# New transpose forms for the q, k, tail and output layouts of a fused attention and channel-mix kernel, with refitted scheduler constants

## Chip, cores and metric

One core of a Trainium2 chip. The metric is the device time of one execution in microseconds (us); medians over the runs of one call. All runs quoted are of the fast state, but for one slow run in f3's median; spans and granted clocks are those of the one core.

## The reference, cut to what matters

```python
# q, k, v: (8 batches, 8 heads, 576 rows, 64), float32
scores = scale * q @ k.T + alibi_bias                  # per batch and head
mask   = (rel >= 0) & (rel < 128)                      # sliding window of 128
attn   = softmax(where(mask, scores, -1e9)) @ v
x      = attn.transpose(0, 2, 1, 3).reshape(8, 576, 512)
# channel mix: x shifted by one row and mixed, then
xk, xr = mu_k * x + (1 - mu_k) * x_prev, mu_r * x + (1 - mu_r) * x_prev
out    = sigmoid(xr @ w_r) * (relu(xk @ w_k) ** 2 @ w_v)
```

## The kernel before

It works on head pairs: 4 groups g in each of 8 batches b. For each pair q and k must be turned so that the head dimension lies on the partitions; scores, exponential (ScalarE), mask (VectorE) and the product with v follow; the attention output must be turned again for the channel mix. A turn is done by TensorE (a transpose is a matmul with the identity, followed by a copy from PSUM) or by the DMA crossbar (a "flip").

The kernel does not list its instructions in their order. It makes a graph of operations, each with a modelled duration, priority, buffers and engines, and a greedy list scheduler orders every engine from these models while the program is built. The built program then holds each engine's instructions in that order.

```python
# the scheduler, cut: an engine that is free takes the first candidate whose buffers are free
if e == "PE":
    cand.sort(key=lambda n: self.pe_key(n, rows))
...
for n in cand:
    if self.take(n):
        break
...
# fitted constants of the schedule
XB = range(5, B)          # q and k of these batches by crossbar
XO = range(6, B)          # attention output of these by crossbar
WIDE = (1,)               # q and k of these by 64x64 quarter transposes
QM, OM = 0, 1             # q, k: full transposes; output: half-height ones
XD, WAIT, XRL = 6, 2.0, 3.0
A = {PE: 14.25, ACT: 4.00, DVE: 4.50, VIR: 0}     # lead of attention over channel mix

# PSUM: two double banks for scores ("duo"), four single ones for all else ("uno")
duo = [pst.tile([128, 2, 512], FP32, name=f"duo{i}") for i in range(2)]
uno = [pst.tile([128, 512], FP32, name=f"uno{i}") for i in range(4)]

# scores of one head pair: two halves, each takes one double bank and is freed by one exponential
s = op(PE, ..., need + [x[5] for x in todo], free)
x = op(ACT, act_t(2 * w), [s], ..., nc.scalar.activation(out=ah(), in_=two(hp)..., func=AF.Exp), (), [hp])

# q and k, full transposes: 8 of 128x128, one single bank, one copy of 1024 columns
def qk_full(b, g, prio):
    hp, hq = Hold(PT), Hold("qk")
    ...
    y = op(ACT, act_t(1024), [t], prio + (3,), lambda e: copy_any(e, qk_buf[hq.idx]..., one(hp)...), (), [hp])

# q and k, quarter transposes: 2 * nr * 4 of 64x64, two single banks, two copies
def qk_quad(b, g, nr, buf, deps, prio, c0, hq, take, free):
    hp = [Hold("p1"), Hold("p1")]
    ...
    ys = [op(QK0 if b == 0 else ACT, {...}, [t], prio + (3,), ..., (), [hp[r]]) for r in range(2)]

# output, half-height transposes: 10 for a head pair, two single banks, two copies (320 + 256)
def out_some(b, g, hx, deps, prio, ht): ...
```

The softmax here doesn't subtract the row's maximum and nothing guards it: scores larger than these inputs give would overflow.

Of the kernel before, what the change touches and what calls it, by code (L numbers as in the profile page):

```python
# [179 lines left out]
def kernel(  # L180
# [12 lines left out]
    nc = tc.nc  # L193

    B, H, S, D = q.shape
    DM = H * D
    DF = moe_w_k.shape[1]
    G = H // 2
    NF = S // 128
# [7 lines left out]
    SM = 128 * NF  # L207
    RELU_SCALE = 0.5 ** 0.5

    PE, ACT, DVE, POOL, SPE, FAB, VIR = "PE", "ACT", "DVE", "POOL", "SP", "FAB", "VIR"  # L210
    NQ, NA, NX, NV, NC = 4, 4, 3, 2, 2
    XB = range(5, B)
    XO = range(6, B)
    X0 = 16
    NWARM = 90
    LOADS = 'v23KtVkabcRWw'
    XD = 6
    OTL = 1.5
    FIN = 384
    RATE = 284.0  # L220
    WIDE = (1,)
    PART_WIDE = True
    QUAD = 0.0565
    RUN = {2: 64 * 284 / 329.0, NF: 128 * 284 / 357.0}
    FLIP = 1.25
    NO = 5
    WAIT = 2.0
    QM = 0
    OM = 1

    def XU(b, g):
        return (DVE,)
# [1 line left out]
    def SQ(order):  # L234
        return (DVE,)

    XT0 = (ACT,)
    QK0 = (ACT, DVE)
    CAST = (DVE,)
    FT = (2, 3)  # L240
    KQ = ACT
    VCUT = True
    XTT = range(6, B)
    MMASK = False
    VDEP = 1
    TCOST = 1.5
# [14 lines left out]
    ts_buf = many(2, [128, H, D], BF16, "ts")  # L261
    tt_buf = many(2, [128, G, 3, 64], BF16, "tt")
# [23 lines left out]
    ident = cst.tile([128, 128], BF16, name="ident")  # L286
# [16 lines left out]
    def one(h):  # L303
        return uno[h.idx if h.cls == "p1" else N1 + h.idx]

    def two(h):
        return duo[h.idx]

    plan = Plan(dict(qx=2, xb=2, p2=2, p1=N1, pt=4 - N1, qk=NQ, at=NA, xu=NX, vs=NV, cb=NC, ts=2, tt=2, xt=2, dl=2, dl0=4,
                     xk=2, rl=3, kk=3, rs=4, ot=NO),  # L310
                {}, WAIT)
# [8 lines left out]
    def dve_t(n, fast=1):  # L320
        return (n / fast + 66) / 960.0

    AHEAD = 30.0
    A = {PE: 14.25, ACT: 4.00, DVE: 4.50, VIR: 0}
    NBIAS = 4
    XRL = 3.0
    MODE = 0
    EARLY = 0.0
    SLOPE = 4.5
# [12 lines left out]
    def op(e, dur, deps, prio, emit, need=(), free=()):  # L342
        prio = rank(prio)
        return plan.add(e, dur, LAT.get(e, 0.2) if isinstance(e, str) else LAT[e[0]] if len(e) == 1 else 0.22,
                        deps, prio, emit, need, free)

    last = {}

    def virtual(key, holds):
        n = plan.add(VIR, 0.0001, 0.0001, [last.get(key)], (0,), None, holds)  # L350
        last[key] = n
        return n
# [11 lines left out]
    def dma(queue, kb, issue, emit, deps=(), need=(), free=(), lat=(1.0, 0.9)):  # L364
        n = plan.add(queue, issue, 0.0, list(deps) + [last.get(queue)],
                     (len(plan.nodes),), emit, need)
        last[queue] = n
        return fab(queue, kb / RATE, n, lat, free)
# [38 lines left out]
    n_ident = dve_op(0.11, emit_ident, [n_iota], (0, -1))  # L407
# [21 lines left out]
    def issue_t(nd):  # L429
        return 0.53 + 0.00034 * nd  # L430
# [16 lines left out]
    def tail_load(b):  # L447
        h = Hold("ts")
        g = virtual("ts", [h])
        ns = []  # L450
        for i in range(2):
            src = (q, k)[i][b, :, SM:S].rearrange("h p d -> p h d")
            ns.append(dma(POOL, 128 * TCOST, issue_t(512), lambda e, i=i, src=src: nc.gpsimd.dma_start(
                out=ts_buf[h.idx][64 * i:64 * i + 64], in_=src), [g]))
        return h, ns
# [66 lines left out]
    th, tl, n_w, src1 = {}, {}, {}, {}  # L522
# [31 lines left out]
    cw, ch, cl, xbh, xbl, tth, ttl, ttg = {}, {}, {}, {}, {}, {}, {}, {}  # L554
# [42 lines left out]
    for (c0, n) in DSEG:  # L597
        n_copy[c0] = dve_op(dve_t(n, 4), lambda e, c0=c0, n=n: nc.vector.tensor_copy(
            out=dist[:, c0:c0 + n], in_=dist[:, 0:n]), [n_dist], (0, 1))
    n_sid = [dve_op(0.1, lambda e, h=h: nc.vector.tensor_scalar(  # L600
        out=sid[:, h], in0=ident, scalar1=-(2.0 ** (-(h + 1))) / scale, scalar2=None,
# [6 lines left out]
    def emit_mu(e):  # L608
# [5 lines left out]
        out=mu_sb.rearrange("p i o -> p (i o)"), in_=one(h_mu)[:, 0:2 * NPO]), (), [h_mu])  # L614
# [12 lines left out]
    def copy_any(e, out, in_):  # L627
        (nc.scalar.copy if e == ACT else nc.vector.tensor_copy)(out=out, in_=in_)  # L628
# [213 lines left out]
            res.append(fab(SPE, 1.0 * rows / 128, n, (1.0, 0.9), [hx]))  # L842
        return res

    def tails(b, prio):
        htt = Hold("tt")
        hs = th[b]
        if b in XTT:
            plan.follow(last["tt"], ttg[b])
            last["tt"] = ttg[b]  # L850
            return tth[b], ttl[b]
        hp = Hold("p1")

        def emit(e):
            for g in range(G):
                nc.tensor.transpose(  # L856
                    one(hp).bitcast(BF16)[:, 128 * g:128 * g + 128],
                    ts_buf[hs.idx][:, 2 * g:2 * g + 2].rearrange("p h d -> p (h d)"), ident)

        def emit_c(e):  # L860
            copy_any(e, tt_buf[htt.idx][:, :, 0:2].rearrange("p g t c -> p g (t c)"),
                     one(hp).bitcast(BF16)[:, 0:128 * G].rearrange("p (g w) -> p g w", g=G))

        t = op(PE, 0.0565 * G, list(tl[b]) + [n_ident], prio + (0,), emit, [hp], [hs])
        g = virtual("tt", [htt])
        c = [op(DVE, dve_t(512), [t, g], prio + (0,), emit_c, (), [hp])]
        return htt, c


# [152 lines left out]
    for part in range(2):  # L1022
        if part == 1:
            htt, n_tt = tails(0, (0, 0, 1, 0))
        for g in range(G):
            prio = (0, 0, part, g)
# [12 lines left out]
            hp = Hold("p1") if part == 0 else None  # L1039
# [29 lines left out]
            for j, (pieces, m0) in enumerate(PART[part]):  # L1069
# [8 lines left out]
            r, hx = attend(0, g, t0, t1, ha, es + vl[0][0:2] + (vl[0][2:] + blank if part else []),  # L1078
                           prio)
# [171 lines left out]
```

## Time and profile before

| | before |
|---|---|
| median of the given runs | 234.99 us (234.88 to 235.05) |
| profile span | 233.1 us |
| TensorE busy | 225.8 us (97%) |
| VectorE, ScalarE busy | 189.8, 160.8 us |
| granted clock | 1.00 |

Matmuls overlap in the pipeline (one of 512 columns is recorded as 380 ns long, and the next starts 216 ns after it), so busy time is not a sum of costs. Throughout I use one account instead. The **priced work** is the sum, over all TensorE groups in their built order, of start-to-start times that the trace shows when nothing waits (216 ns for 512 columns, 109 for 256, 56 for 128, 0.28 us for 32 quarter transposes, 0.16 for ten half ones, 0.25 for a group of the new tail form, 93 ns for each change of array form). The **gaps** are the rest from TensorE's first start to its last, with the last matmul's own price: waits of any kind, and slow matmuls. For the kernel before: 228.8 us = 218.9 priced + 9.95 of gaps.

### The profile page before, as it was taken

What the parts mean: (1) busy time and instruction counts of PE and PEld (TensorE: products, weight loads), DVE (VectorE), ACT (ScalarE), POOL (GpSimd) and SP (SyncE); (2) the same over time, 40 slices, a digit from 0 to 9 for tenths busy, and PEclk for the clock granted to TensorE, in tenths of its full rate; (3) what the DMA queues carried; (4) which work ended last, traced back from release to release, by engine and by line L of the source; (5) the groups of instructions that cost most, each with busy time, mean ns of one, the idle gap of its engine ahead of it and who ended that gap; (6) DMA issues with size and microseconds to landing.
All of it is one profiled execution on the core that took longest, in us unless ns stands there. A gap on an engine that the chain in (4) does not pass through costs nothing.

```text
span 233.1 us, 6268 instructions
## 1 busy us (share of the span) xinstructions
PE 225.8 (97%) x2487; PEld 135.7 (58%) x2487; DVE 189.8 (81%) x427; ACT 160.8 (69%) x292; POOL 97.7 (42%) x124
## 2 busy tenths in 40 slices
PE   7899989999999999999999999999999999999994
PEld 6576765556566765555555755455655844455462
DVE  7587988987797989989989979985769996974242
ACT  3669999759999986984984975947584726326251
POOL 8966773898883893069508935200000000000000
PEclk9999999999999999999999999999999999999999
DMA  7999999999999999989999999993232124121122
GB/s 168 178 167 196 161 162 185 153 199 201 155 154 173 109 138 207 106 106 169 201 188 100 172 181 211 155 146 106 69 89 93 45 48 146 46 90 48 65 70 90
DMA packets 131100, 31.73 MB, mean 136 GB/s; under 512 B 120056, under 2 KB 127232, under 8 KB 131072
## 3 DMA queue, kind: packets, MB, share of 16 engines
q0 software_dynamic: 102736, 16.26, 102.7%
q1 hardware_dynamic: 26592, 14.50, 26.9%
q10 hardware_dynamic: 1744, 0.59, 1.0%
q8 instruction: 19, 0.31, 0.5%
q14 instruction: 9, 0.07, 0.1%
HBM read 33.56 MB, written 9.44 MB: 184 GB/s over the span
## 4 chain that ended last, share of the span: by engine, by line
PE 84%; ACT 5%; DMA 3%; POOL 3%; issue 2%; DVE 1%; DVEq 0%; POOLq 0%; ACTq 0%
PE uno L941 27%; PE uno L907 26%; PE uno L925 14%; PE duo L716 6%; PE duo L658 5%; DMA ts<-in_k_dram 3%; PE uno L771 2%; PE uno L1154 2%; ACT at L672 2%; POOL qx L434 1%; ACT mask L1088 1%; ACT qk L628 1%; PE uno L856 1%; POOL vs L438 1%; ACT rl L914 1%
## 5 line engine op out<-in xcount | busy, mean ns | idle before, releaser
L941 PE MATMUL uno<-wv_sb,kk 128*128 128x512 bf16 (+2 forms) x296 | 71.8, 374 | 0.0
L907 PE MATMUL uno<-xk,wk_sb 128*128 128x256 bf16 (+2 forms) x416 | 69.5, 314 | 0.7 <-ACT rl L914 0.4
L672 ACT ACTIVATE at<-duo 128x1024 bf16<-128x1024 f32 (+2 forms) x68 | 65.7, 1002 | 5.4 <-PE duo L658 5.4
L914 ACT ACTIVATE rl<-uno 128x256 bf16<-128x256 f32 (+2 forms) x104 | 47.3, 492 | 20.3 <-PE uno L907 19.0
L907 PEld LDWEIGHTS <-wk_sb 128*128 128x128 bf16 x416 | 38.7, 98 | 22.1 <-issue 0.9
L685 DVE TENSOR_TENSOR at<-at,mask 128x1024 bf16<-128x1024 bf16 x56 | 37.7, 680 | 8.2 <-ACT at L672 7.8
L438 POOL DMA_DIRECT2D vs<-in_v_dram x32 | 28.4, 895 | 33.9 <-PE duo L716 30.3
L941 PEld LDWEIGHTS <-kk 128*128 128x128 bf16 x296 | 26.4, 98 | 26.2
L880 DVE TENSOR_TENSOR kk<-rl 128x256 bf16<-128x256 bf16 (+2 forms) x104 | 32.8, 334 | 9.0 <-ACT rl L914 7.8
L932 ACT ACTIVATE rs<-uno 128x512 bf16<-128x512 f32 x36 | 22.1, 614 | 26.1 <-PE uno L925 23.1
L925 PE MATMUL uno<-wr_sb,xr 128*128 128x512 bf16 x144 | 37.0, 379 | 0.5 <-ACT rl L914 0.5
L946 DVE SCALAR_TENSOR_TENSOR ot<-rs,uno 128x512 f32<-128x512 bf16 (+2 forms) x37 | 24.6, 668 | 12.1 <-PE uno L941 9.7
L716 PEld LDWEIGHTS <-at 128*128 128x128 bf16 x576 | 21.8, 98 | 6.0 <-issue 0.9
L821 DVE SCALAR_TENSOR_TENSOR xk<-dl,mu_sb,xt 128x576 bf16<-128x576 bf16 (+1 forms) x32 | 24.8, 780 | 0.4
L821 DVE SCALAR_TENSOR_TENSOR xr<-dl,mu_sb,xt 128x576 bf16<-128x576 bf16 (+1 forms) x32 | 24.4, 769 | 0.0
L463 POOL DMA_DIRECT2D cb<-in_k_dram x24 | 21.3, 901 | 7.1 <-DMA wv_sb<-in_moe_w_v_dram 3.3
L628 ACT COPY xt<-uno 128x256 bf16<-128x256 bf16 (+1 forms) x48 | 17.1, 405 | 9.0 <-PE uno L771 8.8
L925 PEld LDWEIGHTS <-xr 128*128 128x128 bf16 x144 | 13.5, 98 | 14.6 <-issue 0.7
L463 POOL DMA_DIRECT2D cb<-in_q_dram x24 | 21.2, 915 | 1.4 <-DMA vs<-in_v_dram 1.2
L628 ACT COPY qk<-uno 128x1024 bf16<-128x1024 bf16 (+2 forms) x26 | 18.8, 777 | 2.4 <-PE uno L1049 0.8
L716 PE MATMUL duo<-vs,at 128*128 128x65 bf16 x448 | 19.1, 193 | 0.0
L814 DVE TENSOR_TENSOR dl<-xt 128x576 bf16<-128x576 bf16 (+1 forms) x32 | 13.7, 434 | 4.2 <-ACT xt L628 4.2
(78 smaller groups left out, 206.8 us busy)
## 6 DMA issues: line engine op xcount, KB each, us to landing
out_dram<-ot SPq DMA_DIRECT2D x30, 256.0 KB, 5.2
vs<-in_v_dram POOLq DMA_DIRECT2D x32, 128.0 KB, 6.6
cb<-in_q_dram POOLq DMA_DIRECT2D x24, 128.0 KB, 7.0
cb<-in_k_dram POOLq DMA_DIRECT2D x24, 128.0 KB, 6.8
out_dram<-ot SPq DMA_DIRECT2D x10, 128.0 KB, 1.8
wk_sb<-in_moe_w_k_dram POOLq DMA_DIRECT2D x2, 512.0 KB, 8.8
wv_sb<-in_moe_w_v_dram POOLq DMA_DIRECT2D x2, 512.0 KB, 10.8
qx<-in_k_dram ACTq DMA_DIRECT2D x4, 128.0 KB, 4.5
```

The source lines that it names most:

```text
L438: return dma(POOL, 256, issue_t(1024), lambda e: nc.gpsimd.dma_start(out=vs_buf[h.idx][:, j, :, 0:D], in_=v[b, :, 128 * j:128 * j + 128].r ...
L463: return [dma(POOL, 256, issue_t(1024), lambda e, r=r: nc.gpsimd.dma_start(out=cb_buf[h.idx][:, i, r], in_=src[:, :, r]), [g]) for r in ra ...
L628: (nc.scalar.copy if e == ACT else nc.vector.tensor_copy)(out=out, in_=in_)
L672: lambda e, ah=ah, w=w, hp=hp: nc.scalar.activation(out=ah(), in_=two(hp)[:, :, 0:w], func=AF.Exp, scale=float(scale)), (), [hp])
L685: nc.vector.tensor_tensor(out=a, in0=a, in1=m, op=ALU.mult)
L716: nc.tensor.matmul(a[:, hl, t - t0], lhsT=at[:, lo:lo + 128], rhs=vs[:, u, 2 * g + hl, :] if u < NF else tvb[:, 2 * g + hl], start=(u == u ...
L821: lambda e: nc.vector.scalar_tensor_tensor(out=buf[hk.idx][:, g, e0 + c0:e0 + c1], in0=dls(), scalar=mu[:, g:g + 1], in1=xc(1), op0=ALU.mu ...
L880: nc.vector.tensor_tensor(out=out, in0=in_, in1=in_, op=ALU.mult)
L907: nc.tensor.matmul(one(hp)[:, 0:n], lhsT=wk_sb[:, po, 128 * fo:128 * fo + 128], rhs=xk_buf[hx.idx][:, po, c0:c1], start=(po == 0), stop=(p ...
L914: a = op(ACT, act_t(n), [s], pr, lambda e, hp=hp, hr=hr: nc.scalar.activation(out=rl_buf[hr.idx][:, 0:n], in_=one(hp)[:, 0:n], func=AF.Rel ...
L925: nc.tensor.matmul(one(hp), lhsT=xr_buf[hx.idx][:, po, 128 * c:128 * c + 128], rhs=wr_sb[:, po], start=(po == 0), stop=(po == NPO - 1))
L941: nc.tensor.matmul(one(hv)[:, a:b], lhsT=kk_buf[hk.idx][:, fo, o:o + 128], rhs=wv_sb[:, fo, a:b], start=(fo == 0), stop=(fo == NFO - 1))
```

## The change

The intent: cheaper q and k loads (512-byte instead of 128-byte pieces) and quarter transposes for batches 1 to 4; full instead of half transposes for the output of these batches; the output of batch 5 moved from TensorE to the crossbar; tails of batches 0 and 1 loaded head-major and turned by 16 matmuls; and refitted constants for the scheduler. The diff, cut:

```diff
-    XO = range(6, B)
+    XO = range(5, B)
-    XD = 6
+    XD = 4
-    WIDE = (1,)
+    WIDE = (1, 2, 3, 4)
+    TW = (0, 1)
-    QUAD = 0.0565
-    RUN = {2: 64 * 284 / 329.0, NF: 128 * 284 / 357.0}
+    QUAD = 0.040
+    RUN = {2: 64 * 284 / 345.0, NF: 128 * 284 / 390.0}
-    WAIT = 2.0
-    QM = 0
-    OM = 1
+    WAIT = 1.0
+    QM = 1
+    OM = 0
-    XT0 = (ACT,)
+    XT0 = (ACT, DVE)
-    XTT = range(6, B)
+    XTT = range(5, B)
-    A = {PE: 14.25, ACT: 4.00, DVE: 4.50, VIR: 0}
+    A = {PE: 10.75, ACT: 10.00, DVE: 3.00, VIR: 0}
-    XRL = 3.0
+    XRL = 4.0
# tail_load: batches in TW are loaded as "h (c r) d -> h c (r d)", r=4
# tails(), for batches in TW:
+            for n in range(8):
+                for hl in range(2):
+                    nc.tensor.matmul(
+                        one(hp)[64 * hl:64 * hl + 64, 64 * n:64 * n + 64],
+                        lhsT=ts_buf[hs.idx][:, n],
+                        rhs=ident.rearrange("p (g t c) -> p t g c", g=G, t=2)[:, hl],
+                        start=True, stop=True)
# ... and two VectorE copies of 256 in place of one of 512 (cut)
```

More of the change, by code (lines that the diff above doesn't have):

```diff
@@ L450, in tail_load @@
         ns = []
+        if b in TW:
+            for i in range(2):
+                ns.append(dma(POOL, 104, issue_t(128), lambda e, i=i: nc.gpsimd.dma_start(
+                    out=ts_buf[h.idx].rearrange("p h d -> p (h d)")[:, 256 * i:256 * i + 256],
+                    in_=(q, k)[i][b, :, SM:S].rearrange("h (c r) d -> h c (r d)", r=4)), [g]))
+            return h, ns
         for i in range(2):
@@ L843, in out_flip, with tails_full @@
         return res
-    def tails(b, prio):
-        htt = Hold("tt")
-        hs = th[b]
-        if b in XTT:
-            plan.follow(last["tt"], ttg[b])
-            last["tt"] = ttg[b]
-            return tth[b], ttl[b]
+    def tails_full(b, prio, htt, hs):
         hp = Hold("p1")
@@ L866, in tails, with emit @@
         c = [op(DVE, dve_t(512), [t, g], prio + (0,), emit_c, (), [hp])]
+        return htt, c
+    def tails(b, prio):
+        htt = Hold("tt")
+        hs = th[b]
+        if b in XTT:
+            plan.follow(last["tt"], ttg[b])
+            last["tt"] = ttg[b]
+            return tth[b], ttl[b]
+        if b not in TW:
+            return tails_full(b, prio, htt, hs)
+        hp = Hold("p1")
+        def emit(e):
+            for n in range(8):
[5 more added lines that the diff above has]
+                        start=True, stop=True)
+        t = op(PE, 0.03 * 16, list(tl[b]) + [n_ident], prio + (0,), emit, [hp], [hs])
+        g = virtual("tt", [htt])
+        c = [op(DVE, dve_t(256), [t, g], prio + (0,), lambda e, i=i: copy_any(
+            e, tt_buf[htt.idx][:, :, i].rearrange("p g (c r) -> p g c r", r=4),
+            one(hp)[:, 256 * i:256 * i + 256].rearrange("p (r g c) -> p g c r", r=4, g=G)),
+                (), [hp]) for i in range(2)]
         return htt, c
```

## The prediction

> **What bounds the kernel now.** I read the page first: busy time by engine, then the windows table, then the groups by form on PE and ACT, the chain that ended last, and the PE timeline.
>
> ```profile
> PE 225.8 (97%) x2487; PEld 135.7 (58%) x2487; DVE 189.8 (81%) x427; ACT 160.8 (69%) x292; POOL 97.7 (42%) x124
> ```
>
> PE is busy for 225.8 of 233.1 us, and the granted clock is 1.00 in every window. The chain that ended last is 84% PE. So the time is the sum of what PE issues, plus its gaps. The windows say where gaps can be (PE, PEld, DVE, ACT, POOL busy, then clock, DMA share, GB/s):
>
> ```profile
> 0.00:20.00 20.00, 18.03 (x264) 12.42 (x264) 14.98 (x64) 12.14 (x23) 15.87 (x27) 1.00 1.52 174
> 20.00:40.00 20.00, 18.18 (x363) 13.88 (x358) 16.75 (x46) 19.19 (x45) 12.45 (x15) 1.00 1.79 174
> 60.00:80.00 20.00, 20.00 (x272) 13.48 (x271) 17.50 (x39) 18.66 (x34) 14.40 (x18) 1.00 2.05 148
> ```
>
> From 40 us on PE is full; before that it lacks about 4 us, and in 20 to 40 us ACT is at 19.19 of 20. The first 25 us also hold 90 filler matmuls. Busy time of pipelined matmuls overlaps, so I cost everything by start-to-start times, which the timeline shows:
>
> ```profile
> 32.35 0.45 PE L1002 MATMUL uno<-ident,cb 64*64 64x64 bf16 x32
> 32.73 1.05 PE L907 MATMUL uno<-xk,wk_sb 128*128 128x256 bf16 x8
> ...
> 38.89 0.32 PE L771 MATMUL uno<-ident,xu 64*128 64x64 bf16 x10
> 39.14 1.04 PE L925 MATMUL uno<-wr_sb,xr 128*128 128x512 bf16 x4
> ...
> 40.97 0.32 PE L771 MATMUL uno<-ident,xu 64*128 64x64 bf16 x10
> 41.13 0.55 PE L658 MATMUL duo<-qk 64*128 64x256 bf16 x8
> ```
>
> Ten half-height output transposes (one head pair) cost 0.16 us when another 64-row form follows (40.97 to 41.13), and 0.25 when a 128-row form follows (38.89 to 39.14): a change of array form costs 0.09 us. Thirty-two quarter transposes, what batch 1 already uses for q and k, take 0.38 with such a change at the end, so 0.29 without.
>
> ```profile
> 66.15 0.61 PE L1154 MATMUL uno<-ident,cb 128*128 128x128 bf16 x8
> 66.60 0.39 PE L856 MATMUL uno<-ident,ts 128*128 128x128 bf16 x4
> 66.82 1.06 PE L1154 MATMUL uno<-ident,cb 128*128 128x128 bf16 x16
> ```
>
> Eight full transposes take 0.45 us, four take 0.22: 56 ns each.
>
> **What the Trainium skill says.** (1) "TensorEngine Tiling (Array Packing)", Key Properties: changing the tiling mode drains TensorE. The trace agrees and gives the size: over all 106 changes of form in the kernel before, the interval exceeds the steady one by a median of 90 to 96 ns by kind of change. (2) "TensorE: Matmul & The Clock Gate", Wait — 56ns, not 53.3ns: a warm matmul costs N / 2.4 GHz plus about 2.5 ns. The trace agrees: median start-to-start is 216 ns at 512 columns, 109 at 256, 56 at 128. (3) Same page, Part 3: matmuls in different tiles of the array overlap, with starts about 4 ns apart. The trace agrees: in a quarter-transpose group three starts follow at 3 to 4 ns, then one at 22. (4) "DMA: Bandwidth & Descriptors", Specifications: at least 512 B is wanted for line rate. The trace's packet records agree in direction: 128 B packets of the software queue took a mean of 35.3 ns, 512 B ones 60.7, so four small ones cost 141 for the bytes of one.
>
> **The change, part by part.** Group counts are from the order of instructions in the two built kernels.
>
> q and k of batches 2 to 4: 12 groups (3 batches, 4 head pairs) of 8 full transposes become 32 quarter ones. 12 x (0.29 - 0.45) = -1.9 us of PE.
>
> Output of batches 1 to 4: 16 groups of ten half transposes become five full ones: 16 x (5 x 0.056 - 0.16) = 16 x 0.12 = +1.9 us.
>
> Output of batch 5: its 4 groups leave PE for the crossbar: -4 x 0.16 = -0.6 us. Its tail transposes leave too: -0.2 us.
>
> Tails of batches 0 and 1: four full transposes (0.22) become 16 matmuls of 64 columns with two column tiles. No row of the trace has this form; if pairs overlap as in (3), 8 pairs at 31 ns (the half transposes' pitch) are 0.25, so +0.05 us in all; if they don't, 16 at 29 ns, +0.5.
>
> Changes of form: 106 before, 110 after: +4 x 0.093 = +0.4 us. The half transposes often sat next to scores in the 64-row form, and the full ones do not; the quarter ones need a form of their own.
>
> Sum on PE: -1.9 + 1.9 - 0.6 - 0.2 + 0.05 + 0.4 = about -0.4 us. Summing every group of both orders with the same prices, unrounded, gives 218.9 and 218.4 us, so -0.5. **The TensorE part is nearly a wash.** The kernel before issued over 228.6 us, so it holds about 9.7 us of gaps over this sum; some 7.5 of these fall before 40 us, including 1.3 of slow first fillers.
>
> ACT, from its groups by form:
>
> ```profile
> L628 ACT COPY qk<-uno 128x1024 bf16<-128x1024 bf16 x12 | 11.9, 1042 | 0.7 <-PE uno L1154 0.7
> L628 ACT COPY xt<-uno 128x320 bf16<-128x320 bf16 x24 | 10.1, 428 | 8.8 <-PE uno L771 8.8
> L628 ACT COPY xt<-uno 128x256 bf16<-128x256 bf16 x24 | 9.1, 382 | 0.3 <-DVE qk L628 0.2
> L628 ACT COPY qk<-uno 128x512 bf16<-128x512 bf16 x10 | 5.7, 619 | 0.8 <-PE uno L1049 0.8
> ```
>
> q and k: 12 x (2 x 0.619 - 1.042) = +2.4 us. Output of batches 1 to 4: 0.428 + 0.382 = 0.81 becomes one copy of 576; by the slope between 512 and 1024 columns I estimate 0.67, so 16 x -0.14 = -2.2. Batch 5: -4 x 0.81 = -3.2. Batch 0: the order shows five of its eight output copies moved to VectorE and one 256-column q/k copy back: -2.0 + 0.4. Sum -4.6 us. Most is beside PE's work and worth nothing. Only the 1.6 us of batch 0 lie in the first 30 us, where ACT is what PE waits for; I count a third to a half, 0.5 to 0.8 us. VectorE gets about 2 us more there, at 15 to 17 of 20 busy: enough room, but less than before.
>
> DMA: a batch of q and k is 8192 packets of 128 B before, 2048 of 512 B after: 8192 x 35.3 / 16 = 18.1 against 7.8 us of engine time. As the DMA share is near 2 when full, wall time is half: 5 us less for each of three batches. This is the largest number here, and I give it nothing: after 40 us PE's list of waits names no DMA. It buys headroom only. The tails of batches 0 and 1 go from 1024 to 256 packets, 2.26 to 0.97 us by the same sum, 0.65 in wall time each. The first is on the chain that ended last:
>
> ```profile
> 8.60 8.04 DMA ts<-in_k_dram
> 18.08 1.30 ACT at L672 x2
> ```
>
> Landing at 16.6 it gates the scores of batch 0's second part. I count half of 0.65, since two VectorE copies follow in place of one and nine fillers now stand just behind in PE's order.
>
> Total: 234.99 - 0.5 (PE) - 0.65 (ACT early) - 0.3 (tails) = 233.5. The priorities and rates of the scheduler were refitted as well, presumably to shorten early gaps, so I shade to **233.3 us**.
>
> **Rivals.** (a) The crossbar becomes a wait. The before kernel flips outputs of batches 6 and 7 when q/k flips are over; now batch 5's five flips (about 1.25 us each on the issuing queue) stand before most of batch 7's q/k flips in an in-order queue, while loads still run. If a flip waits for the last output of batch 5, batch 7's scores come late and PE, in fixed order, stops for 1 to 4 us: 234.5 to 237. For it: the queue order. Against it: these flips land in 2.4 us, and the loads finish some 15 us of DMA time earlier, so the flips start earlier. (b) The freed DMA time does matter, because earlier q and k let attention run ahead and fill the gaps of 20 to 40 us: at most some 3 us of gaps there vanish, 230.5 to 231.5. Against: ACT at 96% limits that window, not loads. (c) Two half-size copies in place of one, with two PSUM banks per quarter-transpose group, make PE wait for a bank: say 12 groups by 0.1 to 0.2, 235 to 236. Batch 1 ran so and did show stalls of 0.4 and 0.5 us behind its groups, but in the ACT-bound window.
>
> **Range and chances.** The counted PE sum is firm to about 0.5 us; the early gaps can give up to 2 us more than I count, and (a) or (c) can cost 2. So 231.5 to 235.3. Faster by 2% needs 230.3, more than half of all gaps gone: 0.04. Slower by 2% needs 4.7 us of new stalls: 0.03. Within 2%: 0.93.
>
> **What would show it right or wrong.** Right: groups of 32 quarter transposes at about 0.29 us apart from the form change, five full ones at 0.28, PE busy about 0.5 us less, the DMA share well below 2 from 40 to 120 us, ACT under 158 us, no wait of PE on DMA after 40 us. The gain, if any, should lie before 40 us: the same point of the channel mix reached about 1 us earlier, and the stretch from there to the end shorter by under 1 us. Wrong: PE waits on crossbar flips, or 20 us windows after 60 with PE under 19.8; tail matmuls at over 0.5 us a group; a gain over 3 us, which would mean that loads had held the early part.

## The result, and the profile after

| | before | changed |
|---|---|---|
| median | 235.02 us (234.88 to 235.27, 4 runs) | 235.99 us (235.78 to 236.21, 4 runs) |
| ratio to before | | 1.0040, 95% interval 1.0023 to 1.0058 |
| profile span | 233.1 | 234.4 |
| priced TensorE work | 218.9 | 218.4 |
| gaps | 9.95 | 11.8 |
| ScalarE, VectorE busy | 160.8, 189.8 | 157.6, 190.6 |

A ratio here is the mean time of one kernel's fast runs over the mean of the other's of the same rounds, so not quite the ratio of the medians. The changed kernel is 0.4% slower: within 2%, as predicted, but on the other side of zero and outside the range (231.5 to 235.3).

First the page's busy line, then the windows (columns as in the prediction: PE, PEld, DVE, ACT, POOL busy, clock, DMA share, GB/s), both of the changed kernel:

```profile
PE 223.9 (96%) x2645; PEld 137.2 (59%) x2675; DVE 190.6 (81%) x432; ACT 157.6 (67%) x276; POOL 85.4 (36%) x112
```

```profile
0.00:20.00 20.00, 18.02 (x273) 13.24 (x273) 15.07 (x66) 10.76 (x20) 15.92 (x27) 1.00 1.47 174
20.00:40.00 20.00, 17.72 (x360) 12.79 (x356) 16.94 (x49) 17.95 (x40) 11.32 (x15) 1.00 1.67 180
40.00:60.00 20.00, 19.27 (x362) 12.87 (x365) 19.40 (x38) 17.61 (x30) 12.91 (x17) 1.00 1.82 195
60.00:80.00 20.00, 18.87 (x341) 11.93 (x343) 17.95 (x37) 18.38 (x32) 10.65 (x14) 1.00 1.31 132
```

The first line is a trap. TensorE seems to have become 1.9 us cheaper, but 2,645 matmuls are recorded against 2,675 weight loads: 30 records are missing, and busy time with them. So I count from starts, aligned with the built order, where a missing record inside a group does no harm. The count gives 230.2 us, 1.4 more than before, while the work is priced 0.5 less. The same reservation holds for the last two windows' PE figures. What can be read from the windows directly is ScalarE: in 20 to 40 us it fell from 19.19 to 17.95, and in 40 to 80 us both ScalarE and VectorE are at 17.6 to 19.4 of 20.

The waits of TensorE, four lines of each list, first before, then changed (us in total, times, longest):

```profile
PE uno L1046 <- DMA qx<-in_q_dram: 0.5, 1, 0.5
PE uno L856 <- issue: 0.5, 1, 0.5
PE uno L925 <- ACT rl L914: 0.5, 1, 0.5
PE uno L907 <- ACT rl L914: 0.4, 1, 0.4
```

```profile
PE duo L665 <- ACT at L679: 1.2, 3, 0.5
PE uno L1075 <- DMA qx<-in_q_dram: 0.7, 1, 0.7
PE uno L954 <- ACT rl L943: 0.5, 1, 0.5
PE uno L936 <- ACT qk L635: 0.4, 1, 0.4
```

The new entry is the first: scores that wait for an exponential of ScalarE (L679), three times. The list of the kernel before has no such line, but a list leaves out short idle times, and the wait itself is not new. Before, the second four of these scores matmuls start at 34.23 us, when the exponential before them has ended, and the eight take 0.86 us instead of 0.56:

```profile
33.71 0.86 PE L658 MATMUL duo<-qk 64*128 64x256 bf16 x8
```

That group costs 0.31 us beyond its price. In the changed kernel two of the three waits are its largest new gaps. Here is the later one in the changed kernel, first TensorE's timeline, then ScalarE's, then the chain that ended last:

```profile
60.89 0.56 PE L665 MATMUL duo<-qk 64*128 64x256 bf16 x8
...
61.43 0.45 PE L1031 MATMUL uno<-ident,cb 64*64 64x64 bf16 x32
61.81 0.40 PE L857 MATMUL uno<-ident,ts 128*128 128x128 bf16 x4
62.05 0.81 PE L936 MATMUL uno<-xk,wk_sb 128*128 128x384 bf16 x4
62.84 0.39 PE L665 MATMUL duo<-qk 64*128 64x256 bf16 x4
63.76 0.34 PE L665 MATMUL duo<-qk 64*128 64x256 bf16 x4 [0.52 <-ACT at L679]
```

```profile
60.42 0.91 ACT L943 ACTIVATE rl<-uno 128x384 bf16<-128x384 f32 x2
61.17 0.69 ACT L635 COPY xt<-uno 128x576 bf16<-128x576 bf16 x1
61.69 2.01 ACT L679 ACTIVATE at<-duo 128x1024 bf16<-128x1024 f32 x2
```

```profile
59.47 1.08 ACT qk L635 x2
60.55 0.78 ACT rl L943 x2
...
61.69 2.01 ACT at L679 x2
```

How to read it: the scores at 60.89 fill both double banks. ScalarE still has two relus and an output copy to do, so their two exponentials run from 61.69 to 63.70. The next scores are due at 62.84; their first half gets the first double bank, their second half stands until 63.76. Beyond the price of its twelve matmuls this scores group cost 0.86 us. At 32.6 us the same picture stands, with a second half copy of q and k (L635) in the place of the output copy, 0.86 us again.

Where the gaps lie, from the account by start times: 0 to 20 us 4.2 before, 4.4 after; 20 to 40 us 3.3 and 3.7; 40 to 70 us 0.65 and 2.3; the rest 1.8 and 1.4.

The DMA side did what it should: for the same 16.26 MB the software queue had 102736 packets and 102.7% of the time of 16 engines before, 83088 packets and 91.7% after.

### The profile page after: what moved, and what is told of

It reads as the page before. It is cut to its first block, busy times and chain, and to the rows that moved or that the text cites. A ratio compares the mean times of both kernels' runs of the same rounds, so it can differ in the third digit from the quotient of the medians.

```text
span 234.4 us, 6591 instructions
## 1 busy us (share of the span) xinstructions
PE 223.9 (96%) x2645; PEld 137.2 (59%) x2675; DVE 190.6 (81%) x432; ACT 157.6 (67%) x276; POOL 85.4 (36%) x112
## 3 DMA queue, kind: packets, MB, share of 16 engines
q0 software_dynamic: 83088, 16.26, 91.7%
## 4 chain that ended last, share of the span: by engine, by line
PE 86%; ACT 6%; DMA 2%; issue 2%; SPq 1%; DVE 1%; DVEq 0%; ACTq 0%
PE uno L970 27%; PE uno L936 25%; PE uno L954 13%; PE duo L665 7%; PE duo L723 6%; ACT at L679 3%; PE uno L761 2%; DMA qx<-in_q_dram 2%; PE uno L1031 2%; ACT qk L635 2%; PE uno L626 1%; PE duo L652 1%; PE uno L723 1%; ACT rl L943 1%; SPq L489 1%
## 5 line engine op out<-in xcount | busy, mean ns | idle before, releaser
L970 PE MATMUL uno<-wv_sb,kk 128*128 128x512 bf16 (+2 forms) x284 | 70.1, 373 | 1.2 <-issue 0.6
L936 PE MATMUL uno<-xk,wk_sb 128*128 128x256 bf16 (+2 forms) x411 | 69.5, 313 | 0.8 <-ACT qk L635 0.4
L679 ACT ACTIVATE at<-duo 128x1024 bf16<-128x1024 f32 (+2 forms) x68 | 63.7, 992 | 7.7 <-PE duo L665 7.7
L943 ACT ACTIVATE rl<-uno 128x256 bf16<-128x256 f32 (+2 forms) x104 | 46.2, 486 | 24.4 <-PE uno L936 21.7
L936 PEld LDWEIGHTS <-wk_sb 128*128 128x128 bf16 x416 | 38.9, 98 | 22.4 <-issue 0.7
L909 DVE TENSOR_TENSOR kk<-rl 128x256 bf16<-128x256 bf16 (+2 forms) x104 | 33.5, 336 | 10.0 <-ACT rl L943 8.0
L954 PE MATMUL uno<-wr_sb,xr 128*128 128x512 bf16 x131 | 35.8, 379 | 1.2 <-ACT rl L943 0.5
L635 ACT COPY qk<-uno 128x512 bf16<-128x512 bf16 (+1 forms) x39 | 20.4, 580 | 2.8 <-PE uno L1031 1.7
L665 PE MATMUL duo<-qk 64*128 64x256 bf16 (+1 forms) x168 | 12.9, 255 | 1.2 <-ACT at L679 1.2
L635 ACT COPY xt<-uno 128x576 bf16<-128x576 bf16 (+2 forms) x19 | 11.5, 607 | 3.0 <-PE uno L761 2.9
L734 DVE TENSOR_TENSOR xu<-duo,rc 128x640 bf16<-128x640 f32 x16 | 13.1, 818 | 0.3 <-PE uno L761 0.2
```

The lines of the kernel that those rows point to most:

```text
L635: (nc.scalar.copy if e == ACT else nc.vector.tensor_copy)(out=out, in_=in_)
L665: nc.tensor.matmul(sa[:, hl, c0:c0 + n], lhsT=kk_, rhs=qq_, start=not bias, stop=True, skip_group_check=True)
L679: lambda e, ah=ah, w=w, hp=hp: nc.scalar.activation(out=ah(), in_=two(hp)[:, :, 0:w], func=AF.Exp, scale=float(scale)), (), [hp])
L909: nc.vector.tensor_tensor(out=out, in0=in_, in1=in_, op=ALU.mult)
L936: nc.tensor.matmul(one(hp)[:, 0:n], lhsT=wk_sb[:, po, 128 * fo:128 * fo + 128], rhs=xk_buf[hx.idx][:, po, c0:c1], start=(po == 0), stop=(p ...
L943: a = op(ACT, act_t(n), [s], pr, lambda e, hp=hp, hr=hr: nc.scalar.activation(out=rl_buf[hr.idx][:, 0:n], in_=one(hp)[:, 0:n], func=AF.Rel ...
```

## The experiments

Fifteen kernels ran, all with correct results. One run of f3 (238.68 us) was slow: its ratio leaves it out, its median does not (235.26 without it). The table gives each one's account; the texts follow. "Priced" and "gaps" are from the profiled run, the stretches are gaps in us of the span.

| kernel | median us (before) | ratio and 95% interval | priced | gaps | 0-20 | 20-40 | 40-70 | rest |
|---|---|---|---|---|---|---|---|---|
| before | 235.02 | | 218.9 | 9.95 | 4.2 | 3.3 | 0.65 | 1.8 |
| changed | 235.99 (235.02) | 1.0040, 1.0023 to 1.0058 | 218.4 | 11.8 | 4.4 | 3.7 | 2.3 | 1.4 |
| e1 | 239.62 (235.17) | 1.0187, 1.0150 to 1.0224 | 218.8 | 15.0 | 4.9 | 4.0 | 2.0 | 4.1 |
| e2 | 239.75 (235.17) | 1.0186, 1.0154 to 1.0218 | 219.7 | 14.2 | 4.7 | 4.4 | 2.2 | 2.9 |
| e3 | 241.42 (235.17) | 1.0253, 1.0215 to 1.0292 | 219.0 | 16.9 | 4.3 | 3.5 | 4.6 | 4.6 |
| e9 | 240.60 (235.17) | 1.0251, 1.0195 to 1.0307 | 218.8 | 18.5 | 4.1 | 3.9 | 2.5 | 8.0 |
| r5 | 235.67 (235.45) | 1.0028, 0.9994 to 1.0063 | 218.4 | 12.8 | 4.2 | 5.3 | 0.9 | 2.4 |
| r6 | 237.66 (235.45) | 1.0096, 1.0073 to 1.0118 | 218.3 | 13.4 | 4.0 | 3.6 | 3.5 | 2.2 |
| r7 | 239.48 (235.45) | 1.0168, 1.0120 to 1.0217 | 218.3 | 15.3 | 4.9 | 3.8 | 2.2 | 4.5 |
| r8 | 236.84 (235.45) | 1.0061, 1.0039 to 1.0083 | 219.3 | 12.3 | 4.4 | 4.9 | 0.7 | 2.3 |
| f1 | 235.04 (235.57) | 0.9979, 0.9957 to 1.0001 | 218.8 | 10.1 | 4.5 | 3.1 | 0.7 | 1.8 |
| f2 | 236.28 (235.57) | 1.0050, 1.0010 to 1.0089 | 218.4 | 11.7 | 4.5 | 3.5 | 2.3 | 1.4 |
| f3 | 235.58 (235.57) | 1.0001, 0.9976 to 1.0027 | 218.4 | 10.9 | 4.5 | 3.3 | 1.4 | 1.8 |
| o1 | 236.68 (235.57) | 1.0044, 1.0013 to 1.0075 | 219.9 | 10.7 | 4.8 | 3.1 | 0.6 | 2.2 |
| s1 | 235.62 (235.15) | 1.0010, 0.9983 to 1.0038 | 218.4 | 10.7 | 4.2 | 3.3 | 1.9 | 1.4 |
| s2 | 240.25 (235.15) | 1.0210, 1.0178 to 1.0242 | 218.4 | 15.8 | 4.1 | 4.3 | 4.5 | 3.1 |
| s3 | 235.66 (235.15) | 1.0019, 0.9992 to 1.0046 | 218.9 | 10.4 | 4.6 | 3.0 | 0.8 | 2.0 |

The gaps of the first 20 us hold the wait for the first f32 load, which varies between the runs (in the lists of waits from no line in r5, r6 and o1 to 1.1 us in e1; 0.5 before, 0.3 in s3, which has the same TensorE instructions); I read nothing from differences of half a microsecond in that column.

A caution on three rows: in r5, r8 and e9 the profiled execution was the slowest of its four (237.15, 237.68 and 243.26 us, against at most 235.81, 236.97 and 240.71 for the others), with a mean granted clock of 0.993. In r5 and r8 the clock fell to 0.66 and 0.69 from 30 to 35 us, so their gaps from 20 to 40 us are in part slow matmuls. The window of r5 (columns as above):

```profile
30.00:35.00 5.00, 4.86 (x77) 3.25 (x78) 3.14 (x9) 4.17 (x8) 3.97 (x5) 0.66 1.42 193
```

Five microseconds at 0.66 lose up to 1.7 us (an estimate from these two numbers).

### First call: the constants, or the operations?

**e1: the changed operations with the constants of before** (XD, QUAD, RUN, WAIT, A and XRL put back).

```diff
-    XD = 4
+    XD = 6
-    WAIT = 1.0
+    WAIT = 2.0
-    A = {PE: 10.75, ACT: 10.00, DVE: 3.00, VIR: 0}
+    A = {PE: 14.25, ACT: 4.00, DVE: 4.50, VIR: 0}
-    XRL = 4.0
+    XRL = 3.0
# QUAD and RUN as well
```

> The changed kernel with the scheduler's constants of the kernel before (priority leads A, WAIT, XRL, XD, QUAD, RUN); all operations stay those of the change. Theory A (the refitted constants place the operations so that TensorE waits for ScalarE between 30 and 70 us): the 1.9 us of extra gaps mostly goes, 234.2 to 234.8. Theory B (the operations themselves, two half copies a group with two banks, make the gaps): stays at 235.6 to 236.4. TensorE's priced work is 218.8 us by its order, 0.4 more than the change's.

Measured: 239.62 us, 1.9% slower than before, with 15.0 us of gaps.

**e2: the operations of before with the constants of the changed kernel** (the reverse edit, without XD).

```diff
-    WAIT = 2.0
+    WAIT = 1.0
-    A = {PE: 14.25, ACT: 4.00, DVE: 4.50, VIR: 0}
+    A = {PE: 10.75, ACT: 10.00, DVE: 3.00, VIR: 0}
-    XRL = 3.0
+    XRL = 4.0
# QUAD and RUN as well
```

> The kernel before with the changed kernel's scheduler constants (A, WAIT, XRL, QUAD, RUN) and none of its operations. Theory A: gaps between 30 and 70 us appear here as well, and the priced TensorE work is 219.7 (0.8 above before), so 236 to 237.5. Theory B: only the 0.8 of priced work shows, 235.5 to 236.

Measured: 239.75 us, as slow as e1. So neither "the constants lose the time, whatever the operations" nor "the operations lose it, whatever the constants" holds: each set of operations runs better with its own fit than with the other's. A mismatch adds 3.2 us of gaps to the changed operations (11.8 to 15.0) and 4.2 to those of before (9.95 to 14.2), while the priced work moves by 0.8 at most.

**e3: before, with wide loads and quarter transposes for batches 1 to 4 and nothing else.**

```diff
-    WIDE = (1,)
+    WIDE = (1, 2, 3, 4)
```

> The kernel before with head-major q and k of batches 1 to 4 alone. Priced TensorE work 219.0, the same as before: 129 changes of form eat the 1.9 us that the quarter transposes save. Theory A (constants): 234.8 to 235.4. Theory B (operations): ScalarE has 12 x 2 half copies in place of 12 whole ones, gaps of 1 to 2 us behind them, 236 to 237.

Measured: 241.42 us, 17 us of gaps. A part of the change done alone is worse than the whole, so parts do not add up. What TensorE waits for longest here is the clue (us in total, times, longest):

```profile
PE uno L856 <- DMA ts<-in_k_dram: 2.5, 2, 2.2
```

The schedule put tail transposes (L856) ahead of a load that had not landed. The cheaper form of the q and k groups is not what these two waits are about. I put them down to the order that came of it; no run tests that for e3.

**e9: changed, with only the three leads A put back.**

```diff
-    A = {PE: 10.75, ACT: 10.00, DVE: 3.00, VIR: 0}
+    A = {PE: 14.25, ACT: 4.00, DVE: 4.50, VIR: 0}
```

> The changed kernel with only the three priority leads A set back (TensorE 14.25, ScalarE 4, VectorE 4.5). Theory A in its narrow form (ScalarE's lead of 10 makes exps and copies run ahead in pairs while TensorE waits for their banks): 234.2 to 234.8, gaps of 40 to 70 us back under 1 us. If another constant or the operations did it: 235.6 or more.

Measured: 240.60 us, so three numbers make a 2% loss. And here the prediction's rival (a), the crossbar wait, does appear, in TensorE's timeline:

```profile
149.65 1.03 PE L936 MATMUL uno<-xk,wk_sb 128*128 128x512 bf16 x4
153.91 0.80 PE L665 MATMUL duo<-qx 64*128 64x256 bf16 x8 [3.23 <-DVE xb L734]
```

Batch 7's scores take q and k from the crossbar (qx). In the issuing queue five output flips, which need VectorE's outputs (xb), stand from 135.0 to 141.8 us, and batch 7's flips only behind them, from 143.1. After the 3.23 us of idle the next matmuls of 512 columns started 426 ns apart for a while, with a granted clock of 0.75 from 155 to 160 us. In the changed kernel this order did not arise.

### Second call: how much do the constants move?

**r5: changed, constants fitted anew by the kernel's own planned end.**

```diff
-    XD = 4
+    XD = 3
-    WAIT = 1.0
+    WAIT = 0.00
-    AHEAD = 30.0
-    A = {PE: 10.75, ACT: 10.00, DVE: 3.00, VIR: 0}
+    AHEAD = 25.00
+    A = {PE: 9.25, ACT: 3.75, DVE: 4.75, VIR: 0}
```

> The changed kernel, every operation kept, with other scheduler constants only (leads 9.25, 3.75, 4.75, WAIT 0, XD 3, AHEAD 25), which the kernel's own plan rates 1.2 us shorter than the changed kernel's (227.9 against 229.1 us at the last matmul). Priced TensorE work 218.4, as in the changed kernel. Theory A (the order that the fit gives makes the gaps, not the operations): gaps fall from 11.8 to about 10, 234.2 to 235.2. Theory B (the operations cost it: two banks per quarter-transpose group, crossbar): gaps stay at 11 or more, 235.6 or more.

Measured: 235.67 us against 235.45, ratio 1.0028 with an interval that holds 1. The gaps from 40 to 70 us shrink from 2.3 to 0.9 us with the same operations, so the operations do not force them. But a new stop stands in the middle of a quarter group (TensorE's timeline):

```profile
28.18 0.35 PE L1031 MATMUL uno<-ident,cb 64*64 64x64 bf16 x19
29.93 0.29 PE L1031 MATMUL uno<-ident,cb 64*64 64x64 bf16 x13 [1.41 <-issue]
```

"issue" is time without a wait that the profile shows. The third call looks at it.

**r6: changed, VectorE's lead 3.00 to 2.75.**

```diff
-    A = {PE: 10.75, ACT: 10.00, DVE: 3.00, VIR: 0}
+    A = {PE: 10.75, ACT: 10.00, DVE: 2.75, VIR: 0}
```

> The changed kernel with VectorE's lead at 2.75 in place of 3.00 and nothing else. Its plan grows from 229.1 to 231.3 us, with the same operations. Theory A: the time follows the plan, 237.5 to 239, all of it in gaps before 100 us. Theory B: a lead that moves by 8% moves nothing of note, 235.7 to 236.5.

Measured: 237.66 us, ratio 1.0096 against the changed kernel's 1.0040: some 1.3 us from one constant moved by a quarter.

**r7: changed without the head-major tails, fitted anew** (TW empty, tail form of before, a scheduler that groups equal forms, other constants).

```diff
-    TW = (0, 1)
+    TW = ()
-        if rows == 64 and n.rows[0] == 64:
+        if rows != 128 and n.rows[0] == rows:
-        t.rows, t.lazy = (64, 64), True
+        t.rows, t.lazy = (65, 65), True
# XD, QUAD, WAIT, AHEAD, A, XRL and SLOPE fitted anew
```

> The changed kernel without its head-major tails (four full transposes and one copy for batches 0 and 1, as before), with the scheduler also pricing the step between 64-row and 64x64 forms, and refitted leads; plan 228.1 us. Priced TensorE work 218.3. If the head-major tails shorten the start as I predicted (0.3 us), the first 20 us hold more gaps than the changed kernel's 4.4 us; if they do nothing, the same. Total by theory A 234.4 to 235.4.

Measured: 239.48 us, with two long stops: 1.7 us at 152 us, in which a product with v waits for VectorE's mask, and 1.4 us at 60 us in the middle of quarter groups, without a wait (the third call looks at such stops). For the tails it says little: gaps of the first 20 us 4.9 against 4.4, within what the f32 load wait varies by. Inconclusive.

**r8: before, VectorE's lead 4.50 to 4.75, same operations.**

```diff
-    A = {PE: 14.25, ACT: 4.00, DVE: 4.50, VIR: 0}
+    A = {PE: 14.25, ACT: 4.00, DVE: 4.75, VIR: 0}
```

> The kernel before with VectorE's lead at 4.75 in place of 4.50 and nothing else. Its plan grows from 228.7 to 229.8 us. Theory A: 235.8 to 237, so a step as large as that from before to after comes of the fit alone. Theory B: 234.9 to 235.3.

Measured: 236.84 us, ratio 1.0061. **The kernel before, with not one operation changed, loses as much from a quarter of one constant as it does from the whole change** (1.0040; the intervals overlap). Its three runs at a clock of 0.999 or more (236.62 to 236.97) all lie above the seven of before (234.86 to 235.76).

### Third call: the stops without a wait, and one price

**f1, f2, f3: before, changed and r5, each with its 90 filler matmuls of 128 columns replaced by 23 of 512** (about the same filler columns, 67 matmuls fewer ahead of the stops).

```diff
+        warms.append(1)
+        if len(warms) % 4 == 1:
+            nc.tensor.matmul(one(h_wm).rearrange("p (a b) -> p a b", a=4), lhsT=warm,
+                             rhs=warm[:, None].to_broadcast([128, 4, 128]), start=True, stop=True)
-        nc.tensor.matmul(one(h_wm)[:, 0:128], lhsT=warm, rhs=warm, start=True, stop=True)
```

> The kernel before with its 90 filler matmuls of 128 columns replaced by 23 of 512 columns at the same places, so the same filler time in 134 fewer TensorE instructions; nothing else. In seven of the ten profiles so far TensorE stops for 0.5 to 1.3 us (1.6 in the refit) with no semaphore to wait for, always at its 956th or 958th instruction, whatever that instruction is; 16 KB transfers on the instruction queue go 256 instructions apart. Theory F (TensorE runs out of fetched instructions, because too many short ones come early): the stop of 0.7 us at instruction 956 goes, 234.0 to 234.6. If the stop has another cause, it stays where the same work is, 234.8 to 235.3.

> The changed kernel with the same wide fillers. Its stop at that place was 0.4 us. Theory F: 235.3 to 235.8, so the step from before to changed stays 1 us or grows. If quarter transposes cost their time through instruction fetch (576 against 192 of them), the changed kernel gains more than the kernel before does.

> The refitted changed kernel (r5) with the wide fillers. Its stop of 1.6 us at instruction 958 in the middle of a group of quarter transposes is the largest term between its plan and its time. Theory F: 234.0 to 234.8, faster than the kernel before. Otherwise 235.4 to 235.8, as r5 was.

Measured: 235.04, 236.28 and 235.58 us against 235.57. In the kernel before the stop looks like this in TensorE's timeline:

```profile
29.53 0.27 PE L856 MATMUL uno<-ident,ts 128*128 128x128 bf16 x2 [0.17 <-ACT qk L628]
30.29 0.27 PE L856 MATMUL uno<-ident,ts 128*128 128x128 bf16 x2 [0.49 <-issue]
```

In f1 it is gone, and the gaps from 20 us to just past this place fall from 1.9 to 1.6. But that is not the fillers' doing, or not shown to be: s3 below has the very TensorE instructions of before, with all its 90 short fillers, and there the stop is gone too, with the same 1.6 us of gaps (in o1 as well, whose TensorE instructions are those of before up to number 1,214). TensorE's timeline of s3:

```profile
29.91 0.42 PE L856 MATMUL uno<-ident,ts 128*128 128x128 bf16 x4 [0.17 <-ACT qk L628]
30.40 1.58 PE L907 MATMUL uno<-xk,wk_sb 128*128 128x256 bf16 x12
```

So the stop comes and goes between executions. In f3 the longest stop is 0.8 us in place of r5's 1.6 (start to start, over the price), and it comes again at TensorE instruction number 957, counting weight loads and matmuls, though 134 instructions fewer stand ahead of the work there: where the stop does come, the place goes by the count, not by the work. The long ones lie at 955 to 957, near 1,723, 1,976 and 3,000, which is three, four and eight times about 255 from the first. Five of the seventeen profiles (e9, f1, o1, s2, s3) have none at the first place. The profile's instruction queue moves blocks of 16 KB, 19 of them before and 21 after, and their starts lie 250 TensorE instructions apart in the mean before.

My guess is that TensorE now and then runs out of fetched instructions at block ends, when short matmuls use them up fast (a quarter group is 64 instructions in 0.28 us). It is not shown, and what decides whether the stop comes stays open. In the two profiles at hand the stop is worth 0.4 us in the changed kernel and 0.7 before, and so does not make the changed kernel the slower one. f2's gaps at 32 and 63 us are unchanged, 0.86 us each. f1 has the lowest ratio, but its interval touches 1, so I don't call it faster.

**o1: before, order kept, every half transposed output (batches 1 to 5, 20 groups) by five full transposes and one copy in place of ten half ones and two copies.** This prices one kind of group without moving anything.

```diff
-        o = op(PE, 0.0295 * m * NJ, deps, prio + (1,), emit, hp, hx)
+        def emit_full(e):
+            for t in range(NJ):
+                nc.tensor.transpose(
+                    one(hp[0]).bitcast(BF16)[:, 128 * t:128 * t + 128],
+                    xu_buf[hx[0].idx][:, t].rearrange("p h d -> p (h d)"), ident)
+        o = op(PE, 0.0295 * m * NJ, deps, prio + (1,), emit_full, hp, hx)
# the first copy takes all 576 columns, the second is not emitted
```

> The kernel before with every engine's order kept, and only the 20 groups of half-height output transposes written as five full ones each with one 576-column copy in place of two. Priced by my steps: 20 x 0.124 more for the transposes less 16 changes of form at 0.093, 219.9 against 218.9, so +1.0 us of TensorE. If the prices hold and nothing else changes: 235.8 to 236.2. If the 2.8 us that ScalarE loses matter: below 235.7.

Measured: 236.68 us; by the ratio 1.0044 that is +1.04 us, where the account has +1.0: 20 groups at +0.124 us are +2.5, and 16 changes of form fewer (90 for 106) are -1.5. The interval of the ratio is +0.3 to +1.8 us, so an agreement to 0.04 us is luck; what it shows is that the price has the right sign and about the right size when the order is kept. ScalarE's smaller number of copies (160.8 to 159.7 us) brought nothing back that shows.

### Fourth call: what makes the two largest gaps

**s1: changed, every engine's order as planned, but two of ScalarE's copies emitted on VectorE at the same place:** the second half copy of q and k at 31.0 us and the output copy at 61.2 us, the two that stand ahead of the late exponentials.

```diff
+                key = n.prio[ACT][1:] if isinstance(n.prio, dict) else None
+                if n.eng == ACT and key in ((0, 1, 0, 2, 3), (0, 2, 0, 1, 1)):
+                    halves_seen[key] = halves_seen.get(key, 0) + 1
+                    if key[-1] == 1 or halves_seen[key] == 2:
+                        n.eng = DVE
                 n.emit(n.eng)
```

> The changed kernel, every engine's order as planned, except that two of ScalarE's copies are done by VectorE at the same place in the plan: the second half copy of head pair 2 of batch 1 (31.0 us) and the output copy of head pair 1 of batch 2 (61.2 us). If ScalarE's backlog makes the gaps of 0.86 us at 32.6 and 62.8 us, each shrinks by 0.4 to 0.6 us, and the total by about 1 us (ratio to before near 1.000). If the order of TensorE alone makes them, or VectorE's added 0.6 us each only carries the wait on, the gaps move or stay and the time is within 0.3 us of the changed kernel's (ratio near 1.004).

Measured: the two gaps fall from 0.86 us each to 0.46 and 0.47, all gaps from 11.8 to 10.7 us, the span from 234.4 to 233.4. TensorE and ScalarE of s1, at the place shown above:

```profile
60.20 0.56 PE L665 MATMUL duo<-qk 64*128 64x256 bf16 x8
...
61.35 0.81 PE L936 MATMUL uno<-xk,wk_sb 128*128 128x384 bf16 x4
62.10 0.86 PE L665 MATMUL duo<-qk 64*128 64x256 bf16 x8
```

```profile
59.73 0.91 ACT L943 ACTIVATE rl<-uno 128x384 bf16<-128x384 f32 x2
60.63 1.94 ACT L679 ACTIVATE at<-duo 128x1024 bf16<-128x1024 f32 x2
```

The exponentials start 0.43 us after the earlier scores, not 0.80. The line of scores that wait on L679 is gone from the list of waits, but only because what is left is short: the eight scores matmuls at 62.10 stand in one row, yet take 0.86 us where those at 60.20 take 0.56. The median is 235.62 us at a ratio of 1.0010, against the changed kernel's 1.0040. The intervals of the two ratios overlap, so the total is only suggestive, while the effect on the two gaps is shown. (The profiled run of s1 is the fastest of its six, that of the changed kernel the slowest of its four, so their spans overstate the step; the ratios say 0.7 us.) Of the 1.1 us in the account 0.8 are these two gaps and 0.2 lie in the first 10 us, which the edit doesn't touch.

**s2: the same, with all sixteen second half copies of batches 1 to 4 on VectorE.** The edit is that of s1 with another set of keys: `[(0, b, 0, g, 3) for b in WIDE for g in range(G)]`.

> The changed kernel, order as planned, with the second half copy of all sixteen quarter groups of batches 1 to 4 on VectorE: ScalarE loses 9.8 us, VectorE gains about 9.8 us (some 200 busy of 234). If ScalarE's backlog is the cause, the gaps before exponentials between 30 and 90 us go and up to 1.5 us come back. If VectorE, already at 18 to 19 of 20 us there, turns into the bound, new waits on VectorE's copies, masks and reciprocals cost 1 us or more (237 or slower).

Measured: 240.25 us. ScalarE falls to 150.5 us, VectorE rises to 199.1, and TensorE's longest waits are now on VectorE's copies. So moving ScalarE's work is not a gain in itself: here the time lost on VectorE's copies is larger than anything that ScalarE's relief brought. This run can't say what the relief alone is worth, since it loads VectorE at the same time.

**s3: before, order kept, the copy of 1024 columns done as two of 512.**

```diff
-        y = op(ACT, act_t(1024), [t], prio + (3,), lambda e: copy_any(
-            e, qk_buf[hq.idx].rearrange("p t (c r) -> p t c r", r=NF), ...
+        y = op(ACT, act_t(1024), [t], prio + (3,), lambda e: [copy_any(
+            e, qk_buf[hq.idx][:, t].rearrange("p (c r) -> p c r", r=NF), ...) for t in range(2)], (), [hp])
```

> The kernel before, order kept, in which the copy of 1024 columns behind the full q and k transposes of batches 2 to 4 is done as two of 512 columns: ScalarE +12 x (2 x 0.61 - 1.04) = +2.2 us, TensorE unchanged. If splitting the copies costs the changed kernel its gaps (rival c of the prediction, its ScalarE part), this loses 0.5 to 1.5 us against before. If ScalarE has room after 40 us, as the prediction counted, within 0.2 us of before (ratio 0.999 to 1.001).

Measured: 235.66 us, ratio 1.0019 with an interval that holds 1; the gaps from 40 to 70 us go from 0.65 to 0.8. My expectation of +2.2 us for ScalarE was too high: its busy time rose by 0.6 (two copies in a row overlap at their ends, so the mean duration of one counts the overlap twice). Splitting the copies by itself does not make the gaps, in the order of before; on the clock the upper limit leaves room for 1.1 us.

## Why the prediction was wrong

**The step that failed is the gap term.** The prediction took the gaps of before as the start and let them shrink: -0.65 us for ScalarE, -0.3 for the tails, -0.2 for the new constants. They grew by 1.9 us.

**TensorE's priced work: right.** Predicted -0.5 us; counted in the trace of the changed kernel -0.5 (218.9 to 218.4). That is the same sum over the same built order, so the test lies in the prices. Groups of 32 quarter transposes took 0.29 us, as said (61.43 to 61.81 above, less 0.09 for the change of form; the account keeps 0.28). The new tail form, the one price without a row, took 0.374 us from its start to the next group's in both places, so 0.28 without the change of form, where I had estimated 0.25 (the account keeps 0.25, so 0.06 us of the gaps are this). And o1 bears out the price of the largest added term on the clock: +1.04 us, interval +0.3 to +1.8, for +1.0.

**The early relief of ScalarE, -0.65 us: failed.** ScalarE did lose work in 20 to 40 us (19.19 to 17.95), and its total fell by 3.2 us where I had said 4.6. But the gaps from 20 to 40 us went from 3.3 to 3.7. I had reasoned from a busy share: an engine at 96% in a window where TensorE lacks time must be what TensorE waits for. The list of before shows what TensorE waited for on ScalarE there: two relus, 0.9 us in all, and no output copy. What counts is where ScalarE's backlog stands when a bank is wanted, and the new order put a copy ahead of an exponential at 32 us. s1 shows this by moving that one copy; o1, which takes copies away elsewhere, shows no gain from it.

**The tails, -0.3 us: not seen.** The first 20 us hold 4.4 us of gaps against 4.2. A gain of 0.3 would be hidden under the f32 load's wait, and r7 could not settle it.

**The gaps of before as the base, with a shade of -0.2 us for the refitted constants: this is the error that cost most.** I took the gaps as a property of the kernel that a refit shortens. The refit did shorten those of the changed operations (e1 to changed: 15.0 to 11.8 us), but from a base that I had not counted. The constants and the operations together decide the order, and the order decides the gaps, to within one or two microseconds and more: r8 moves before by +1.4 us with no operation changed, r6 moves the changed kernel by some +1.3, e9 by some +5 with three leads, and r5 has it at a ratio whose interval holds 1. In place of -0.95 us (0.65 and 0.3) the gaps gave **+1.9 us**, and 1.6 of these lie between 40 and 70 us, where I had called TensorE full and looked no further. The gap of 0.86 us at 63 us alone takes its window below 19.8 of 20, which I had named as a sign of being wrong. The range fell with it: two microseconds to each side were mostly kept for (a) or (c) and for early gains, not for a new order's gaps.

**The rivals.** (c), a wait for banks at 235 to 236 us, came nearest in size, and the two largest new gaps are waits for a bank that ScalarE frees late. Its detail is mostly wrong, though: the banks are the double ones of the scores, not the single ones of the quarter groups, and the copy that is late in the second case is an output copy. Single banks do show once with a sizeable gap: the wait of L936 for a half copy of q and k in the list above, at 46.55 us, is 0.55 us start to start over the price, and s1 has it as well; before, the largest wait of this kind is 0.37, at 54.29 us. s3 adds that splitting copies makes no gap of note in the old order. (a), crossbar waits, is absent from the changed kernel (its gaps from 140 to 160 us are 0.2 us in all, as before) and appears only in e9. (b), gains from earlier loads, is not seen; the software queue lost 11 points of its share with nothing gained, as predicted.

**A check that was open to me.** The kernel's scheduler gives a planned end of TensorE when it is built: 228.7 us for before and 229.1 for changed. Its own model of the work leaves 3.6 and 5.4 us of gaps in them, so the added gaps were already in the plan. The plans of e1, e2 and e3 hold most of their losses too: 232.8, 232.0 and 232.6. Not that a plan ranks kernels well: r5 is planned at 227.9 and runs as before does; e9 at 230.3 and runs at 240.6, with a crossbar wait of 3.2 us in its profile. But a plan that says "no gain" was evidence that I did not use.

**What stays open.** Which part of the change owns the new gaps can't be said, since operations and fit come as a pair (e1, e2, e3). Outside the two gaps that s1 halved, the change of order is named as a cause because nothing else differs in r6 and r8, not because each gap was traced. With the two halved, 10.7 us of gaps are left against 9.95 before, and these 0.8 us are not explained (s3, with TensorE's order of before, has 10.4, so half of it may be no more than the spread of single profiles). No version of either kernel was shown to be faster than before; the best, f1, is at 0.9979 with an upper limit of 1.0001.

## What to carry to other kernels

Where a scheduler orders the engines from fitted constants, a change of operations has two effects: the price of the operations, which can be worked out to a few tenths of a microsecond and tested with the order kept, and the order, which must be given its own width (here one to two microseconds from the smallest nudges) and tested by nudging a constant of the old kernel. An engine at 96% in a window is a bound only if its queue holds up something that TensorE wants there: look at what stands ahead of the operation that frees the bank. A stop that vanishes in one profile proves little until another execution of the same instructions is looked at. And compare the counts of matmuls and weight loads before reading busy time, because missing records look like a gain.

## What the Trainium skill lacked or had wrong

- "Runtime: NRT & Kernel Launch", Instruction fetch mechanics, has the 16 KiB blocks of 256 instructions, which the trace agrees with (16 KB blocks, 250 counted TensorE instructions apart in the mean), but calls the cost of a block's end mostly hidden. Here TensorE stopped without a wait for 0.2 to 1.4 us by the timeline's idle time (0.49 before, 1.41 in r5) at instruction numbers some 255 or multiples of it apart. If these are block ends, which is not shown, the cost is not always hidden; it was hidden in s3, with the same TensorE instructions as before.
- "TensorEngine Tiling (Array Packing)", Key Properties, says that a change of tiling mode drains TensorE, without a size: 0.09 us for each of 106 to 110 changes here, some 10 us of the kernel. Nor does it give the time of a run of small tiles: 32 transposes of 64x64 took 0.28 to 0.29 us, ten of half height 0.16, and 16 matmuls of 128x64 0.28. (The 4 ns between tiles that the prediction cites from another page holds within a set of four; from one set to the next it was 22 ns.)
